# A spectral mixer and a gated feed-forward on one core: two transform stages and the first batch in plain float32, the weights' conversion on VectorE, mixed rows moved from SBUF to SBUF

## The chip, the cores and the metric

One core of a Trainium2 chip runs the whole program. The core has five engines that the text speaks of by the profile's names: PE (TensorE, which multiplies matrices; PEld is its loading of the stationary operand), DVE (VectorE), ACT (ScalarE), POOL (GpSimd) and SP (SyncE, which here issues every DMA). The metric is device time in microseconds (us), the median of several executions.

## The reference

```python
X = np.fft.rfft(x, axis=1)                      # x: [8 batches, 3008, 256] float32
Yr = Xr @ w_r - Xi @ w_i + b_r
Yi = Xr @ w_i + Xi @ w_r + b_i
Y  = soft_threshold(Yr, 0.01) + 1j * soft_threshold(Yi, 0.01)
y  = np.fft.irfft(Y, n=3008, axis=1)            # [8, 3008, 256] = 24064 tokens of 256
h  = y @ w_in                                   # w_in: [256, 2048] float64
out = (h * sigmoid(1.702 * h)) @ w_out          # w_out: [2048, 256] float64, out float32
```

The two feed-forward weights come as float64 bits, and the kernel turns them into float32 on the chip.

## The kernel before

**Precision.** Almost every product is made of float32r operands, a float32 type of shorter mantissa that the PE multiplies in one pass. To keep float32's accuracy each operand is cut in two parts: `split(hi, lo, src)` (L124) lets ACT cast `src` into `hi` and lets DVE subtract, `lo = src - hi`. `mm3` (L128) then issues three matmuls into the same PSUM bank: hi x hi (L129), hi x lo (L130) and lo x hi (L131).

**The spectral part of one batch** (`spectral`) is a Fourier transform of 3008 = 64 x 47 points in steps:

- stage A (16 times a batch): `load_x`, `split_x`, then `stage_a`, the transform of length 47 as one `mm3` of 512 columns; the result goes through ACT to a DRAM buffer `s1`.
- stage B (12 times, each for a pair of k2): `load_b` reads a matrix `kr` and rows `br` of `s1`, `split_b` splits `br`, `stage_b` is the transform of length 64. The matrix `kbs` holds its high and its low part side by side, so that each of four products is one matmul of 256 columns (L272) and one of 128 (L273); the correction part of the bank is copied by ACT (L277) and added to the main part by DVE (L278).
- the mix (12 times): `stage_mix`, six `mm3` of 256 columns, then on DVE bias and threshold (L294 to L296), and on POOL the subtraction (L297). The rows `mv` are then written to a DRAM buffer `yd` (two DMAs) and read back as `yr` in another order of partitions (one DMA, `load_y`).
- the inverse of length 64 (12 times): `split_y`, then `stage_inv`, one `mm3` of 512 columns; ACT evicts it and it goes to the DRAM buffer `s2`.

**Tokens.** `load_u` reads 96 rows `ur` of `s2`, `split_u` splits them and `tokens(u)` (128 times in all) makes the last transform, of length 47, and 188 tokens at a time: four matmuls of 188 columns (L372) and four of 94 (L373) into two banks, ACT's copy (L375) and DVE's addition (L376) into `yf`, and a split of `yf` into the token tiles `th`, `tl`.

**Feed-forward.** For each of 47 tiles of 512 tokens and each of 8 quarters q of 256 hidden units, `Ffn.up` makes four `mm3` of 512 columns (`pa<-th,wi_h` and the like), the gate on ACT (L408), and splits `hb`/`lb` and `ht`/`lt`; `Ffn.down` makes seven `mm3` of 256 columns into the accumulator `po`. That is 12 matmuls of 512 columns and 21 of 256 for each of 376 pairs of tile and quarter.

**The weights' conversion** runs once at the start, for each q `up_weights` and `down_weights` (two halves). `from_float64` (L166) loads 512 KB of float64 and turns the bits: DVE L177, L178, L180 and L183, ACT L179 and L184, and on POOL two multiplications (L182, L185). `up_weights` adds a subtraction and an addition on POOL (L193, L194); `down_weights` six sums on POOL (L202 to L207) and a split.

**Order.** Each engine runs its own instructions strictly in the order in which the program's scheduler put them; a waiting instruction holds up what stands behind it on its engine. The program first runs all of batch 0's spectral part; the weights of q = 0 to 4 are converted meanwhile, and those of q = 5 to 7 are held back until the last mix of batch 0 (`tc.issue_after(mixed[0, 11])`, L461). Then follow four stage A of batch 1, the first three calls of `tokens`, and the feed-forward, in which the spectral parts of batches 1 to 7 fill in. PSUM has four banks that all but `po` share (`bank`, L115). In SBUF, seven tiles with the tag `w2` serve most of the spectral part.

Of the kernel before, what the change touches and what calls it, by code (L numbers as in the profile page):

```python
# [37 lines left out]
def halves(v):  # L38
    """v as the sum of two values of 12 significant bits."""
    def r12(u):  # L40
        m, e = np.frexp(u)
# [4 lines left out]


def constants():
# [7 lines left out]
    # DFT-47: rows (n2, p), columns (k2, re | im, p)  # L56
# [5 lines left out]
    # +1 where the bin of (k1, k2) is kept by rfft, -1 where its conjugate is  # L62
# [24 lines left out]
    # inverse DFT-47: rows (k2, re | im, p), columns (p, n2)  # L87
# [5 lines left out]

    pack = np.zeros((128, 928), np.float32)
    pack[:96, 0:192] = np.concatenate(halves(a), 1)
    pack[:, 192:704] = np.concatenate([h[i] for h in halves(np.stack([binv, binv0])) for i in range(2)], 1)
    pack[:96, 704:892] = np.concatenate(halves(ai), 1)
    pack[:, 892:916] = 1.0
    pack[N1:, 892:916] = sign
# [4 lines left out]
def fourier_mix_then_gated_ffn(ctx: ExitStack, tc: tile.TileContext, x, w_r, w_i, b_r, b_i, w_in, w_out, pack, kbs, out):  # L104
# [37 lines left out]
    wf_h = cst.tile([128, 3, 2, D], F32R, name="wf_h")
    wf_l = cst.tile([128, 3, 2, D], F32R, name="wf_l")

    def later_constants():
# [8 lines left out]
        split(wf_h[:, 2], wf_l[:, 2], wr)
        for i, op in ((0, ALU.add), (1, ALU.subtract)):
            t = buf2("wd")
            nc.vector.scalar_tensor_tensor(t, wr, -1.0, wi, ALU.mult, op)
# [8 lines left out]
    def from_float64(src):  # L166
        """(a, e): a + e is the float64 value; below float32's normal range -> 0."""
# [8 lines left out]
        v = nc.vector  # L176
        v.tensor_scalar(a, w1, 3, 0x3FFFFFF8, ALU.logical_shift_left, ALU.bitwise_and)  # L177
        v.scalar_tensor_tensor(a, w1, -0x40000000, a, ALU.bitwise_and, ALU.bitwise_or)  # L178
        nc.scalar.activation(m, w1f, AF.Abs)  # L179
        v.tensor_scalar(m, m, TINY, None, ALU.is_ge)  # L180
        af, ef = a.bitcast(F32), e.bitcast(F32)
        nc.gpsimd.tensor_tensor(af, af, m, ALU.mult)  # L182
        v.tensor_scalar(e, a, -0x800000, None, ALU.bitwise_and)  # L183
        nc.scalar.activation(m, w0, AF.Copy, scale=2.0 ** -52)  # L184
        nc.gpsimd.tensor_tensor(ef, ef, m, ALU.mult)  # L185
        return af, ef

    def up_weights(q):
# [4 lines left out]
        nc.gpsimd.tensor_tensor(a, a, hi.bitcast(F32), ALU.subtract)  # L193
        nc.gpsimd.tensor_tensor(lo, e, a, ALU.add)  # L194
# [349 lines left out]
```

## Time and profile before

| | |
|---|---|
| median of 3 runs | 2728.8 us (2728.42 to 2730.14) |
| span of the profiled execution | 2728.8 us |
| mean granted PE clock of the profiled execution | 0.983 |
| PE busy | 2614.7 us (96%), 16624 matmuls |
| DVE busy | 2333.5 us (86%) |
| ACT busy | 1830.1 us (67%) |
| POOL busy | 314.0 us (12%) |

The profiled execution's time is its span, 2728.8 us, and there is nothing around it that the page shows. An engine's busy time is the union of its instructions. Matmuls overlap each other in the record, so what one matmul costs is read from the distance of two starts, not from its duration.

### The profile page before, as it was taken

The page shows a single profiled execution, that of the slowest core. Times are in us where ns is not written, and L with a number is a line of the kernel's source. Part 1 is how long each engine was busy: PE and PEld are TensorE (multiplying, and loading weights), DVE is VectorE, ACT ScalarE, POOL GpSimd, SP SyncE. Part 2 cuts the span into 40 slices and gives each one's busy share as a digit, 9 for nine tenths or more (in the row PEclk, how much of TensorE's full clock was granted, in tenths as well). Part 3 has the DMA queues.
Part 4 walks back from the last instruction along what each step waited for, and adds up shares of the span by engine and source line. Part 5 has one row for each costly group of instructions (what it writes and reads, how often), then busy time and mean ns, then how long its engine had stood idle before and what let it go on. Part 6 is the DMA issues. An engine that isn't in the chain of part 4 may idle for free.

```text
span 2728.8 us, 44465 instructions
## 1 busy us (share of the span) xinstructions
PE 2614.7 (96%) x16624; PEld 2351.6 (86%) x16624; DVE 2333.5 (86%) x3885; ACT 1830.1 (67%) x3190; POOL 314.0 (12%) x243
## 2 busy tenths in 40 slices
PE   4759999999999999999999999999999999999998
PEld 2639988899889998899988998889998898999997
DVE  7988998889888988789888999879898799877776
ACT  6557667767677666766668666766667666666564
POOL 6660110010000100001000100000010011000000
PEclk9769999999999999999999999999999999999999
DMA  6553334223242222422233222322224223200000
GB/s 212 165 158 101 92 89 117 89 83 86 67 126 81 83 82 78 123 77 75 75 108 110 68 75 80 118 86 79 76 79 130 72 68 91 82 30 31 17 22 16
DMA packets 181897, 238.53 MB, mean 87 GB/s; under 512 B 17200, under 2 KB 116272, under 8 KB 181680
## 3 DMA queue, kind: packets, MB, share of 16 engines
q1 hardware_dynamic: 181680, 235.69, 29.5%
q8 instruction: 130, 2.13, 0.3%
q14 instruction: 87, 0.71, 0.1%
HBM read 135.48 MB, written 100.14 MB: 86 GB/s over the span
## 4 chain that ended last, share of the span: by engine, by line
PE 62%; DVE 2%; ACT 1%; issue 1%; DMA 0%; DVEq 0%; SPq 0%; ACTq 0%
PE pa L129 11%; PE pa L130 11%; PE pa L131 11%; PE po L129 8%; PE po L130 8%; PE po L131 8%; PE pa L372 1%; PE pa L272 1%; PE pa L373 1%; ACT gb L408 0%; PE pa L273 0%; DVE gt L417 0%; DVE lt L126 0%; ACT hb L125 0%; DVE lb L126 0%
## 5 line engine op out<-in xcount | busy, mean ns | idle before, releaser
L408 ACT ACTIVATE gb<-pa 128x512 f32<-128x512 f32 x752 | 445.5, 597 | 417.7 <-PE pa L131 414.3
L129 PE MATMUL pa<-th,wi_h 128*128 128x512 f32 x1504 | 595.7, 396 | 9.8 <-ACT th L125 4.3
L126 DVE TENSOR_TENSOR lt<-gt,ht 128x1024 fp32r<-128x1024 f32 x376 | 465.8, 1239 | 161.3 <-ACT ht L125 160.5
L130 PE MATMUL pa<-tl,wi_h 128*128 128x512 f32 x1504 | 591.3, 393 | 0.0
L131 PE MATMUL pa<-th,wi_l 128*128 128x512 f32 x1504 | 588.1, 391 | 0.0
L125 ACT CAST ht<-gt 128x1024 fp32r<-128x1024 f32 x376 | 394.5, 1049 | 109.0 <-DVE gt L419 105.3
L130 PE MATMUL po<-lt,wo_h 128*128 128x256 f32 x1504 | 430.7, 286 | 1.2 <-DVE lt L126 1.2
L129 PE MATMUL po<-ht,wo_h 128*128 128x256 f32 x1504 | 428.7, 285 | 0.9 <-ACT ht L125 0.9
L131 PE MATMUL po<-ht,wo_l 128*128 128x256 f32 x1504 | 426.4, 283 | 0.0
L126 DVE TENSOR_TENSOR lb<-gb,hb 128x768 fp32r<-128x768 f32 x376 | 365.2, 971 | 68.9 <-ACT hb L125 66.0
L125 ACT CAST hb<-gb 128x768 fp32r<-128x768 f32 x376 | 314.6, 837 | 68.6 <-PE po L131 64.8
L129 PEld LDWEIGHTS pa<-th,wi_h 128*128 128x128 f32 x1504 | 284.0, 189 | 61.9 <-ACT gb L408 6.8
L129 PE MATMUL po<-hb,wo_h 128*128 128x256 f32 x1128 | 325.1, 288 | 11.0 <-DVE o L443 8.5
L131 PEld LDWEIGHTS pa<-th,wi_l 128*128 128x128 f32 x1504 | 283.2, 188 | 59.3
L130 PEld LDWEIGHTS pa<-tl,wi_h 128*128 128x128 f32 x1504 | 284.2, 189 | 43.4
L131 PE MATMUL po<-hb,wo_l 128*128 128x256 f32 x1128 | 320.5, 284 | 0.0
L130 PE MATMUL po<-lb,wo_h 128*128 128x256 f32 x1128 | 320.4, 284 | 0.0
L297 POOL TENSOR_TENSOR mv<-mv,mt 128x512 f32<-128x512 f32 x96 | 154.7, 1611 | 1322.2 <-DVE mt L296 1094.8
L417 DVE TENSOR_TENSOR gt<-gb 128x512 f32<-128x512 f32 x376 | 270.7, 720 | 33.7 <-ACT gb L408 28.8
L130 PEld LDWEIGHTS po<-lt,wo_h 128*128 128x128 f32 x1504 | 288.3, 192 | 9.3 <-DVE lt L126 1.6
L131 PEld LDWEIGHTS po<-ht,wo_l 128*128 128x128 f32 x1504 | 288.4, 192 | 7.1
L129 PEld LDWEIGHTS po<-ht,wo_h 128*128 128x128 f32 x1504 | 287.7, 191 | 7.7 <-ACT ht L125 1.1
(95 smaller groups left out, 5155.6 us busy)
## 6 DMA issues: line engine op xcount, KB each, us to landing
xr<-in_x SPq DMA_DIRECT2D x128, 192.0 KB, 3.1
kr<-in_kbs SPq DMA_DIRECT2D x96, 256.0 KB, 2.9
s<-aev SPq DMA_DIRECT2D x128, 192.0 KB, 2.3
br<-s SPq DMA_DIRECT2D x96, 256.0 KB, 3.0
yd<-mv SPq DMA_DIRECT2D x192, 128.0 KB, 2.4
yr<-yd SPq DMA_DIRECT2D x96, 256.0 KB, 2.9
s<-iev SPq DMA_DIRECT2D x96, 256.0 KB, 2.2
ur<-s SPq DMA_DIRECT2D x128, 192.0 KB, 2.8
```

What stands on the lines that cost most here:

```text
L125: nc.scalar.copy(hi, src)
L126: return nc.vector.tensor_tensor(lo, src, hi.bitcast(F32), ALU.subtract)
L129: nc.tensor.matmul(ps, lhsT=wh, rhs=xh, start=start, stop=False)
L130: nc.tensor.matmul(ps, lhsT=wh, rhs=xl, start=False, stop=False)
L131: nc.tensor.matmul(ps, lhsT=wl, rhs=xh, start=False, stop=stop)
L272: nc.tensor.matmul(pv[:, c, :], lhsT=bh[:, i, cs], rhs=kb[:, i], start=True, stop=False)
L297: nc.gpsimd.tensor_tensor(v, v, t, ALU.subtract)
L372: nc.tensor.matmul(pv[:, j, :], lhsT=uh[:, j, cs], rhs=kz, start=True, stop=False)
L373: nc.tensor.matmul(pv[:, j, :94], lhsT=ul[:, j, cs], rhs=kz[:, :94], start=False, stop=True)
L408: nc.scalar.activation(o, ps.rearrange("p (h n) -> p h n", h=2), AF.Gelu_apprx_sigmoid)
L417: nc.vector.tensor_tensor(gt[:, 0:2], b12, gb[:, 0:3:2], ALU.subtract)
```

## The change

Four things change.

1. **Batch 0's spectral part is made of plain float32 matmuls**: stage A, stage B, the mix and the inverse take the float32 tiles as they are, without `split` and with one matmul for each `mm3`. In `split_y` only ACT's scaling by the sign is left. The float32r parts of the constants are made for the later batches in `split_constants`.
2. **Stage B and `tokens` are plain float32 in every batch**: stage B is four matmuls of 128 columns into one bank, `tokens` four matmuls of 94 columns into one bank; the correction parts, their copies and additions, and the splits of `br` and `ur` are gone. `tokens` splits its PSUM bank straight into `th`, `tl`. The matrix `kr` is half as large.
3. **The weights' conversion** keeps on POOL only the six sums of `down_weights`. The comparison and multiplication that were L180 (DVE) and L182 (POOL) become one fused DVE instruction (new L186); L185, L193 and L194 become DVE instructions (new L190, L198, L199).
4. **Mixed rows** go from `mv` to `yr` by four DMAs from SBUF to SBUF; `yd` and `load_y` are gone.

```diff
 def later_constants():
...
+        for tag, op in (("ht", ALU.add), ("th", ALU.subtract)):
+            t = buf([128, 2, D], F32, "wd", tag=tag)
             nc.vector.scalar_tensor_tensor(t, wr, -1.0, wi, ALU.mult, op)
+            wf32.append(t)
+        wf32.append(wr)
+
+    def split_constants():
+        split(ka[:, 0], ka[:, 1], ka32)
+        split(ki[:, 0], ki[:, 1], ki32)
+        for v in range(3):
+            split(wf_h[:, v], wf_l[:, v], wf32[v])
...
 def from_float64(src):
...
+        nc.scalar.activation(m, w1f, AF.Abs)
         v.tensor_scalar(a, w1, 3, 0x3FFFFFF8, ALU.logical_shift_left, ALU.bitwise_and)
         v.scalar_tensor_tensor(a, w1, -0x40000000, a, ALU.bitwise_and, ALU.bitwise_or)
-        nc.scalar.activation(m, w1f, AF.Abs)
-        v.tensor_scalar(m, m, TINY, None, ALU.is_ge)
         af, ef = a.bitcast(F32), e.bitcast(F32)
-        nc.gpsimd.tensor_tensor(af, af, m, ALU.mult)
+        v.scalar_tensor_tensor(af, m, TINY, af, ALU.is_ge, ALU.mult)
         v.tensor_scalar(e, a, -0x800000, None, ALU.bitwise_and)
+        m = buf([128, 2, 256], F32, "wm", tag="lt")
         nc.scalar.activation(m, w0, AF.Copy, scale=2.0 ** -52)
-        nc.gpsimd.tensor_tensor(ef, ef, m, ALU.mult)
+        v.tensor_tensor(ef, ef, m, ALU.mult)
...
 def up_weights(q):
...
-        nc.gpsimd.tensor_tensor(a, a, hi.bitcast(F32), ALU.subtract)
-        nc.gpsimd.tensor_tensor(lo, e, a, ALU.add)
+        nc.vector.tensor_tensor(a, a, hi.bitcast(F32), ALU.subtract)
+        nc.vector.tensor_tensor(lo, e, a, ALU.add)
...
 def stage_a(q):
...
-            mm3(ps[:96], ka[:, 0], ka[:, 1], *xs.pop(q))
+            if b == 0:
+                nc.tensor.matmul(ps[:96], lhsT=ka32, rhs=xs.pop(q), start=True, stop=True)
+            else:
+                mm3(ps[:96], ka[:, 0], ka[:, 1], *xs.pop(q))
...
 def stage_b(sp):
...
+            pv = bank().rearrange("p (c v i n) -> p c v i n", c=2, v=2, i=2)
             for i in range(2):
-                pv = bank().rearrange("p (c n) -> p c n", c=2)
                 for c in range(2):
                     cs = slice(128 * c, 128 * c + 128)
-                    nc.tensor.matmul(pv[:, c, :], lhsT=bh[:, i, cs], rhs=kb[:, i], start=True, stop=False)
-                    nc.tensor.matmul(pv[:, c, :128], lhsT=bl[:, i, cs], rhs=kb[:, i, :128], start=False, stop=True)
...
+                    nc.tensor.matmul(pv[:, c, :, i], lhsT=t[:, i, cs], rhs=k[:, i], start=True, stop=True)
+            nc.scalar.copy(co[:, :, 0:2], pv.rearrange("p c v i n -> p c v (i n)"))
             nc.vector.tensor_tensor(co[:, :, 2], co[:, :, 0], co[:, :, 1], ALU.add)
+            z = co.rearrange("p c v n -> p (c v) n")
+            if b == 0:
+                zs[sp] = z
+                return
...
 def stage_mix(sp):
...
+                    if b == 0:
+                        nc.tensor.matmul(ps, lhsT=z[:, 3 * c + v], rhs=wf32[v][:, c], start=c == 0, stop=c == 1)
+                    else:
...
             nc.gpsimd.tensor_tensor(v, v, t, ALU.subtract)
+            y = ys[sp] = buf2("yr")
             for i in range(2):
-                nc.sync.dma_start(yd[2 * sp + i].rearrange("r k e -> k r e"), v[64 * i:64 * i + 64])
-
-        def load_y(sp):
-            ys[sp] = buf2("yr")
-            nc.sync.dma_start(ys[sp], yd[2 * sp:2 * sp + 2].rearrange("s r k e -> (r k) s e"))
+                for r in range(2):
+                    nc.sync.dma_start(y[64 * r:64 * r + 64, i], v[64 * i:64 * i + 64, r])
...
 def stage_inv(sp):
...
+            if b == 0:
                 for i in range(2):
-                    mm3(pv[:, i], ki[:, 0, 1 - i], ki[:, 1, 1 - i], yh[:, i], yl[:, i])
+                    nc.tensor.matmul(pv[:, i], lhsT=ki32[:, sp == 0 and i == 0], rhs=y[:, i], start=True, stop=True)
...
 def tokens(u):
-        uh, ul = us.pop(u)
...
+        t = us.pop(u)
+        pv = bank()[:, :2 * JP].rearrange("p (c n) -> p c n", c=2)
         for c in range(2):
...
             for j in range(2):
...
+                nc.tensor.matmul(pv[:, c, 94 * j:94 * j + 94], lhsT=t[:, j, 128 * c:128 * c + 128], rhs=kz, start=True, stop=True)
...
-            split(th[:, :, at:at + n], tl[:, :, at:at + n], yf[:, :, o:o + n])
+            split(th[:, :, at:at + n], tl[:, :, at:at + n], pv[:, :, o:o + n])
```

On PE, one call of `tokens` in the feed-forward, before (uh and ul are the parts of the loaded rows, kz the transform's matrix):

```order
L372 MATMUL pa<-kz,uh 128x188
L373 MATMUL pa<-kz,ul 128x94
L372 MATMUL pa<-kz,uh 128x188
L373 MATMUL pa<-kz,ul 128x94
L372 MATMUL pa<-kz,uh 128x188
L373 MATMUL pa<-kz,ul 128x94
L372 MATMUL pa<-kz,uh 128x188
L373 MATMUL pa<-kz,ul 128x94
L129 MATMUL pa<-th,wi_h 128x512
```

and in the changed kernel, between a mix and the feed-forward (kc is the tile of constants, ur the loaded rows):

```order
L131 MATMUL pa<-wf_l,zh 128x256
L132 MATMUL pa<-wf_h,zl 128x256
L370 MATMUL pa<-kc,ur 128x94 x4
L131 MATMUL po<-lb,wo_h 128x256
L132 MATMUL po<-hb,wo_l 128x256
```

Eight float32r matmuls of 188 and 94 columns became four float32 matmuls of 94; stage B's eight (256 and 128 columns) became four of 128 in the same way.

On POOL, the weights of q = 5 behind the last mix of batch 0, before (wa, we and wm are `from_float64`'s a, e and m; w is `down_weights`' tile):

```order
L297 TENSOR_TENSOR mv<-mv,mt 128x512 x8
L182 TENSOR_TENSOR wa<-wa,wm 128x512 x2
L185 TENSOR_TENSOR we<-we,wm 128x512
L193 TENSOR_TENSOR wa<-wa,wi_h 128x512
L185 TENSOR_TENSOR we<-we,wm 128x512
L194 TENSOR_TENSOR wi_l<-we,wa 128x2x256
L202 TENSOR_TENSOR w_1414<-we,wa 128x2x128
L202 TENSOR_TENSOR w_1414<-we,wa 128x256
```

and on DVE at that place in the changed kernel:

```order
L298 TENSOR_TENSOR mv<-pa,mv 128x512
L183 TENSOR_SCALAR wa<-wraw 128x512 x2
L299 TENSOR_SCALAR mt<-mv 128x512
L184 SCALAR_TENSOR_TENSOR wa<-wraw,wa 128x512 x2
L186 SCALAR_TENSOR_TENSOR wa<-wm,wa 128x512
L187 TENSOR_SCALAR we<-wa 128x512
L190 TENSOR_TENSOR we<-we,wm 128x512
L198 TENSOR_TENSOR wa<-wa,wi_h 128x512
L186 SCALAR_TENSOR_TENSOR wa<-wm,wa 128x512
L199 TENSOR_TENSOR wi_l<-we,wa 128x2x256
L187 TENSOR_SCALAR we<-wa 128x512
```

The six multiplications, subtractions and additions of a q that POOL made now stand in DVE's queue: six instructions more there, and two (L180) fewer. In the changed order the weights of q = 0 to 2 and most of q = 3 also stand ahead of the first addition of stage B (new L275) on DVE.

More of the change, by code (lines that the diff above doesn't have):

```diff
@@ L71, in constants @@
     b = np.stack([np.block([[c, -s * sign[:, k]], [s, c * sign[:, k]]]) for k in range(NS)])
-    b = np.stack(halves(b), 2).reshape(NS // 2, 2, 2 * N1, 4 * N1).transpose(0, 2, 1, 3)
+    b = b.reshape(NS // 2, 2, 2 * N1, 2 * N1).transpose(0, 2, 1, 3)
     w0r, w0i = np.zeros(N1), np.zeros(N1)
@@ L92, in constants @@
     ai = ai.reshape(96, 94)
[L94 to L99, printed above, removed]
+    pack = np.zeros((128, 470), np.float32)
+    pack[:96, 0:96] = a
+    pack[:, 96:224] = binv
+    pack[:, 224:352] = binv0
+    pack[:96, 352:446] = ai
+    pack[:, 446:470] = 1.0
+    pack[N1:, 446:470] = sign
     return pack, b.astype(np.float32)
@@ L249, in load_b, with stage_b @@
             raw[sp] = t, k
[L251 removed]
+        def stage_b(sp):
             if sp == 0:
@@ L315, in stage_inv @@
         def stage_inv(sp):
-            yh, yl = ys.pop(sp)
+            y = ys.pop(sp)
             pv = bank().rearrange("p (s d) -> p s d", s=2)
-            if sp == 0:
+            if b == 0:
                 for i in range(2):
-                    mm3(pv[:, i], ki[:, 0, 1 - i], ki[:, 1, 1 - i], yh[:, i], yl[:, i])
+                    nc.tensor.matmul(pv[:, i], lhsT=ki32[:, sp == 0 and i == 0], rhs=y[:, i], start=True, stop=True)
+            elif sp == 0:
+                for i in range(2):
+                    mm3(pv[:, i], ki[:, 0, 1 - i], ki[:, 1, 1 - i], y[0][:, i], y[1][:, i])
             else:
-                mm3(pv, ki[:, 0, 0], ki[:, 1, 0], yh, yl)
+                mm3(pv, ki[:, 0, 0], ki[:, 1, 0], *y)
             ev = buf2("iev")
@@ L336, in spectral @@
         steps.append((4000, lambda: None))
-        for n in range(12 + 5):
-            add(0, split_b, n, 12)
+        for n in range(12 + 4):
             add(900, stage_b, n, 12)
             add(2000, stage_mix, n - 1, 12)
-            add(0, load_y, n - 3, 12)
-            add(0, split_y, n - 5, 12)
-            add(650, stage_inv, n - 5, 12)
+            add(0, split_y, n - 4, 12)
+            add(650, stage_inv, n - 4, 12)
         return steps
@@ L468, in fourier_mix_then_gated_ffn @@
             spec.pop(0)[1]()
-    done, ready = 0, 0
+    done = 0
     def tokens_to(n):
-        nonlocal done, ready
+        nonlocal done
         while done < NB * NU and JP * done < n:
-            while ready < min(done + 2, NB * NU) and JP * ready < n:
-                load_u(ready + 1)
-                split_u(ready)
-                ready += 1
+            load_u(done)
+            load_u(done + 1)
             tokens(done)
```

79 lines of the change are left out of this document (25 added, 54 removed).

## The prediction

> **What bounds the kernel now.** I read the 40 slices of the page first, then the chain that ended last, then the stretches of the start, then who makes PE wait.
>
> ```profile
> PE   4759999999999999999999999999999999999998
> POOL 6660110010000100001000100000010011000000
> PE 62%; DVE 2%; ACT 1%; issue 1%; DMA 0%; DVEq 0%; SPq 0%; ACTq 0%
> ```
>
> From the fourth slice on PE is full and the last chain is PE alone; in the first three PE is half idle and POOL is busy. The stretches (each row: length, then busy time of PE, PEld, DVE, ACT, POOL, granted clock):
>
> ```profile
> 0.00:55.60 55.60, 25.59 (x48) 11.36 (x48) 41.91 (x47) 32.85 (x59) 38.09 (x32) 1.00 0.74 229
> 55.60:143.00 87.40, 63.57 (x339) 56.26 (x339) 85.45 (x129) 49.93 (x97) 53.15 (x44) 0.84 0.57 164
> 143.00:191.00 48.00, 20.60 (x49) 11.26 (x50) 44.37 (x53) 26.36 (x52) 40.27 (x33) 0.53 0.55 164
> ...
> 250.00:2728.80 2478.80, 2445.94 (x15851) 2221.39 (x15849) 2116.16 (x3583) 1674.27 (x2903) 179.11 (x131) 1.00 0.27 80
> ```
>
> Two regimes, then. From 250 us PE is idle for 2478.8 - 2445.9 = 33 us in all. Before 191 us DVE is the fullest engine (85.45 of 87.4 in batch 0's stages B to inverse), and in the third stretch POOL with DVE. The rows that mark the stretches: on PE the first stage B, the last inverse and the first feed-forward matmul; on DVE the first weight instruction and the last mix; on POOL the first weight work after that mix, and the end of it.
>
> ```profile
> 55.64 0.79 PE L272 MATMUL pa<-kb,bh 128*128 128x256 f32 x2 [7.87 <-ACT bh L125]
> 157.19 0.79 PE L129 MATMUL pa<-yh,ki 128*128 128x512 f32 x1 [3.71 <-ACT yh L311]
> 190.77 1.22 PE L129 MATMUL pa<-th,wi_h 128*128 128x512 f32 x2 [4.26 <-ACT th L125]
> ```
>
> ```profile
> 13.02 0.42 DVE L177 TENSOR_SCALAR wa<-wraw 128x512 int32<-128x512 int32 x1
> ...
> 143.61 0.68 DVE L295 TENSOR_TENSOR mv<-pa,mv 128x512 f32<-128x512 f32 x1
> ```
>
> ```profile
> 148.66 2.86 POOL L182 TENSOR_TENSOR wa<-wa,wm 128x512 f32<-128x512 f32 x2
> 194.13 0.46 POOL L207 TENSOR_TENSOR w<-w 128x128 f32<-128x128 f32 x1
> ```
>
> The last three q take POOL from 148.7 to 194.6, 15.3 us each, and the feed-forward begins under their end. So the change has two terms: how much earlier than 190.8 the feed-forward can begin, and what PE's work costs after it, where nearly every microsecond counts.
>
> **Term 1, the start.** POOL's rows for the weights:
>
> ```profile
> L185 POOL TENSOR_TENSOR we<-we,wm 128x512 f32<-128x512 f32 x16 | 25.9, 1619 | 4.2 <-DVE we L183 2.5 <-ACT co L277 1.3 <-ACT wm L179 0.4
> L182 POOL TENSOR_TENSOR wa<-wa,wm 128x512 f32<-128x512 f32 x16 | 24.5, 1535 | 22.7 <-DVE wm L180 15.6 <-DVE wa L178 5.6 <-DMA kr<-in_kbs 1.4
> L194 POOL TENSOR_TENSOR wi_l<-we,wa 128x512 fp32r<-128x512 f32 x8 | 13.8, 1719 | 0.1
> L193 POOL TENSOR_TENSOR wa<-wa,wi_h 128x512 f32<-128x512 f32 x8 | 12.2, 1530 | 0.0
> ```
>
> These 76.4 us of 131.5 (the three stretches) leave POOL; 55 us stay. What they cost on DVE I bound by DVE's means in the start, while POOL is busy, and by single instructions and steady means without it:
>
> ```profile
> L178 DVE SCALAR_TENSOR_TENSOR wa<-wraw,wa 128x512 int32<-128x512 int32 x16 | 14.5, 910 | 0.2
> L183 DVE TENSOR_SCALAR we<-wa 128x512 int32<-128x512 int32 x16 | 14.8, 929 | 1.2 <-POOL wa L182 1.2
> L177 DVE TENSOR_SCALAR wa<-wraw 128x512 int32<-128x512 int32 x16 | 11.2, 697 | 0.6 <-POOL w L202 0.6
> L126 DVE TENSOR_TENSOR wo_l<-w,wo_h 128x896 fp32r<-128x896 f32 x8 | 11.3, 1418 | 0.9 <-ACT wo_h L125 0.9
> L126 DVE TENSOR_TENSOR xl<-xr,xh 96x512 fp32r<-96x512 f32 x30 | 28.5, 963 | 11.0 <-ACT xh L125 11.0
> ...
> 37.73 0.41 DVE L183 TENSOR_SCALAR we<-wa 128x512 int32<-128x512 int32 x1
> ...
> L126 DVE TENSOR_TENSOR bl<-br,bh 128x512 fp32r<-128x512 f32 x81 | 55.4, 684 | 11.8 <-ACT bh L125 11.5
> ...
> L296 DVE TENSOR_SCALAR mt<-mv 128x512 f32<-128x512 f32 x14 | 5.8, 417 | 0.0
> ```
>
> A q is now two of each of L177, L178, the fused one (not in the trace; priced as L178, also a fused instruction on the same shape), L183 and L190, and one each of L198, L199 and the split. With POOL busy: 2 x (0.70 + 0.91 + 0.91 + 0.93 + 0.96) + 2 x 0.96 + 1.42 = 12.2 us. Without: 2 x (0.41 + 0.68 + 0.68 + 0.41 + 0.68) + 2 x 0.68 + 1.0 = 8.1 us (1.0: the split's 1.42 scaled as 0.963 goes to 0.684). POOL's share of the start falls from 131.5/191 = 69% to about 55/146 = 38%, so I take 9.5, somewhat nearer the lower bound. The Trainium skill (SBUF — State Buffer, SBUF: two separate sides) has VectorE and GpSimd taking turns at a shared port, the loser blocked for the whole instruction. The 0.41 beside a mean of 0.93 agrees; by that rule POOL's remaining 55 us are the most that DVE can lose.
>
> Now in DVE's order:
>
> 1. *To stage B.* The first weight instruction ran at 13.0 us, after the first load; the constants' three subtractions and two fused sums cost 3 x 0.96 + 2 x 0.91 = 5 us; ahead of the first new L275 stand 7.6 halves of 4.75 us = 36. Sum 54 us (bounds 49 to 64). Stage A is covered: it loses `split`, PE needs 16 x 0.92 = 15 us, and only its evictions and loads remain, interleaved with the weights on ACT. Without that cover its way through `s1` would show, which is the 7.87 us that PE waits ahead of 55.64.
> 2. *Twelve pairs.* DVE per pair: an addition of at most 0.68 and the mix, 2 x 0.68 + 0.42, 2.5 us, times 12 plus 2.4 halves of weights = 41. PE per pair, by the prices of term 2: 4 x 0.23 + 6 x 0.46 + 2 x 0.46 = 4.6, times 12 = 55, plus 2 to fill: last mix at 111 us against 143.6 now. PE takes over as the bound here. (At a clock of 0.84 it would be 9 us more; with PE full I expect 1.00, as after 200 us.)
> 3. *To the feed-forward.* Three q of 9.5 us plus six `xl` of 0.68 = 33: 144, and some 2 us of `tl` and the first matmul: 146. Under this cover lies the last pair's way to `s2` and back: now the last inverse begins 157.2 - 143.6 = 13.6 us after the last mix, with the two DMA steps below in it; one fewer (2.9), the inverse (0.9) and two more such steps (5.3) make 17 us, which would show only if the weights took less than that.
>
> The SBUF to SBUF exchange drops one of two DMA steps:
>
> ```profile
> yd<-mv SPq DMA_DIRECT2D x192, 128.0 KB, 2.4
> yr<-yd SPq DMA_DIRECT2D x96, 256.0 KB, 2.9
> ```
>
> SP issues four DMAs for three; the first waits for POOL as `yd`'s did, with the next `kr`, `br` and `s2` behind it. Later batches read `yr` long after; I price it at 0 beyond the 17 us above.
>
> Term 1: 146 - 191 = **-45 us**. With lower bounds everywhere (49 + 2, the pairs at DVE's 39, then 24 + 4 + 2): 120, -71; with upper bounds (64 + 57 + 5 for the clock, then 37 + 4 + 2): 169, -22.
>
> **Term 2, PE after the start.** Starts of float32r matmuls in the steady part, two neighbours of 512 and of 256 columns, and the ends of a `tokens` half and of a stage B:
>
> ```profile
> 1012.74 0.40 PE L129 MATMUL pa<-th,wi_h 128*128 128x512 f32 x1
> 1012.97 0.39 PE L130 MATMUL pa<-tl,wi_h 128*128 128x512 f32 x1
> ...
> 1015.04 0.28 PE L131 MATMUL po<-ht,wo_l 128*128 128x256 f32 x1
> 1015.16 0.28 PE L129 MATMUL po<-ht,wo_h 128*128 128x256 f32 x1
> ...
> 1010.07 0.25 PE L372 MATMUL pa<-kz,uh 96*128 96x188 f32 x1
> 1010.63 0.28 PE L130 MATMUL po<-lb,wo_h 128*128 128x256 f32 x1
> ...
> 1017.17 0.28 PE L272 MATMUL pa<-kb,bh 128*128 128x256 f32 x1
> 1018.21 0.28 PE L129 MATMUL po<-hb,wo_h 128*128 128x256 f32 x1
> ```
>
> 512 columns cost 0.23, 256 cost 0.12. Between 1010.07 and 1010.63 lie four `tokens` matmuls and one of 256: 0.56 - 0.12 = 0.44, 0.11 each though they have 188 or 94 columns. Stage B's eight: 1.04 - 0.12 = 0.92, 0.115 each. So below 256 columns the price is that of a stationary load, about 0.115, whatever the columns. What a plain float32 matmul costs no row shows. From below: one load and pass, 0.115. From above: four products of halves, each with its own load, 0.46. Between: two loads (high and low stationary half), 2 x 0.115 = 0.23; and four products by columns at 128 are 512 columns, also 0.23. I take 0.23 for 128 and 94 columns, and by columns 0.46 for 256 and 0.92 for 512.
>
> Stage B: 4 x 0.23 = 0.92 against 0.92: 0 for 84 pairs. `tokens`: 0.92 against 0.88, 125 times: +5 us. Bounds: one load, -(0.46 x 84 + 0.42 x 125) = -91; four, +(0.92 x 84 + 0.96 x 125) = +197.
>
> The Trainium skill (FP8 and Floating Point Precision, TensorE Precision Notes) counts four passes of the array for true FP32; read as columns that is the sum taken, read as four whole matmuls it is the first rival.
>
> **Term 3, waits of PE.** DVE loses, after 250 us,
>
> ```profile
> L126 DVE TENSOR_TENSOR ul<-ur,uh 96x512 fp32r<-96x512 f32 x121 | 82.7, 684 | 0.7 <-ACT uh L125 0.3
> L376 DVE TENSOR_TENSOR yf<-pa,yf 128x188 f32<-128x188 f32 x244 | 78.6, 343 | 4.0 <-ACT yf L375 3.8
> L278 DVE TENSOR_TENSOR co<-pa,co 128x256 f32<-128x256 f32 x166 | 66.9, 417 | 13.5 <-ACT co L277 13.0
> ```
>
> and `bl`'s 55.4: 284 of 2116 us. That is off PE's path; it can shorten only the 33 us in which PE waits. I take a quarter, -8 (bounds 0 and -33).
>
> Sum against the profiled 2728.8, which is also the median: 2728.8 - 45 + 5 - 8 = **2681 us**.
>
> **Rivals.**
>
> *Float32 costs PE more than 0.23 below 256 columns.* The place is stage B and `tokens` in the full part, 836 matmuls; the gain of 48 is gone when each costs 48/836 = 0.06 more, at 0.29. For it: a stationary load's own record is 0.19 (192 ns) against a step of 0.115,
>
> ```profile
> L130 PEld LDWEIGHTS po<-lt,wo_h 128*128 128x128 f32 x1504 | 288.3, 192 | 9.3 <-DVE lt L126 1.6
> ```
>
> and two halves could fail to hide behind each other: 0.38 each gives (1.52 - 0.92) x 84 + (1.52 - 0.88) x 125 = +130 in place of +5: 2806. Four loads give 2873. Against it: loads of float32r overlap well. Chance 0.17.
>
> *VectorE's conversion stays at its slow means.* For it: POOL's sums and subtractions still run beside it. Term 1 -22: 2704. Chance 0.18.
>
> *The start shrinks further and the waits go:* weights at 8.1 us a q, but the pairs still at PE's 55 (49 + 2 + 55 + 30 = 136, -55), and term 3 at -28: 2651. For it: DVE's single instructions of 0.41. Against it: DVE would then be next to full for 130 us, with ACT's casts between its steps. Chance 0.12.
>
> *One load suffices for float32:* 2728.8 - 45 - 91 - 8 = 2585. Against it: then splitting would gain nothing, and the halves' products must come from somewhere. Chance 0.03.
>
> **How the numbers follow.** The forecast has 0.48, and 0.02 stay for a float32 price close to 0.29, no change. Faster by over 0.2% (5.5 us, about what a measurement tells from no change): 0.48 + 0.18 + 0.12 + 0.03 = 0.81; the same 0.02; slower 0.17. The range reaches from 2640, midway between the third rival and all lower bounds together (2728.8 - 71 + 5 - 33 = 2630), to 2735, into the first rival; below it lies some 0.06, above it 0.14.
>
> **What would show it.** First feed-forward matmul near 146 us; last mix near 111; DVE full from 111 to 144. Four L370 or L273 followed by the next matmul within 0.92 + 0.12 us. PE idle after the start about 25 us, DVE near 1850. Wrong if the groups of four float32 matmuls take over 1.2 us, or if the feed-forward begins after 170 us.

## The result and the profile after

The changed kernel takes **2644.6 us** (median of 4 runs, 2643.55 to 2644.80) against 2729.5 for the kernel before, run beside it (4 runs, 2728.42 to 2730.44): ratio **0.9689**, 95% interval 0.9675 to 0.9703, or 85 us less. The forecast was 48 us less. The profiled execution has a span of 2642.9 us and a mean granted clock of 0.986; below, spans are compared with spans.

The slices and the chain of the changed kernel's page:

```profile
PE   6799999999999999999999999999999999999998
POOL 3401110001000100000100100000100010000000
PE 94%; DVE 2%; DMA 1%; ACT 1%; issue 1%; SPq 0%; POOL 0%; DVEq 0%; ACTq 0%; POOLq 0%
```

PE is now full from the third slice on, and POOL does little even at the start. I cut both traces at the first feed-forward matmul. The kernel before, the two stretches (length, then busy time of PE, PEld, DVE, ACT, POOL with their instructions, granted clock, DMA share, GB/s):

```profile
0.00:190.77 190.77, 109.53 (x436) 78.65 (x436) 171.49 (x229) 109.02 (x207) 131.27 (x107) 0.81 0.61 183
190.77:2728.80 2538.03, 2505.17 (x16189) 2272.99 (x16189) 2162.04 (x3657) 1721.10 (x2984) 182.77 (x137) 1.00 0.28 80
```

The changed kernel, the start in its three steps (to the first stage B, to the last mix, to the feed-forward), then the rest:

```profile
0.00:45.00 45.00, 23.94 (x33) 7.00 (x33) 31.62 (x51) 25.30 (x43) 12.97 (x20) 0.72 0.90 283
45.00:105.50 60.50, 54.99 (x274) 47.29 (x275) 40.68 (x69) 27.81 (x51) 24.66 (x26) 0.93 0.60 171
105.50:138.60 33.10, 17.88 (x52) 10.50 (x50) 31.07 (x48) 20.62 (x37) 13.57 (x17) 0.60 0.71 215
138.60:2642.90 2504.30, 2487.87 (x16189) 2264.40 (x16189) 1904.69 (x3030) 1530.00 (x2357) 170.32 (x134) 1.00 0.23 68
```

So the 86 us between the spans are two amounts: the feed-forward begins **52 us** earlier (138.6 against 190.8), and the part after it is **34 us** shorter (2504.3 against 2538.0) with the same number of matmul records, 16189. Half of these 34 is PE's idle time (32.9 to 16.4), half is PE's busy time (2505.2 to 2487.9). In both kernels 6.2 us of the idle time come after the last matmul, so the gaps between matmuls fell from 26.7 to 10.2 us.

The marks of the start in the changed kernel's timeline, on PE the first stage B, the last inverses, the first `tokens` and the first feed-forward matmul:

```profile
44.93 3.76 PE L273 MATMUL pa<-kr,br 128*128 128x128 f32 x16 [9.87 <-DMA br<-s]
...
113.35 2.17 PE L327 MATMUL pa<-yf,kc 128*128 128x256 f32 x4 [2.79 <-ACT yf L312]
...
132.05 5.44 PE L370 MATMUL pa<-kc,ur 96*128 96x94 f32 x24
138.62 1.22 PE L130 MATMUL pa<-th,wi_h 128*128 128x512 f32 x2 [1.14 <-ACT th L126]
```

then ACT's first copy of stage B, and on DVE the first addition of stage B and the last mix:

```profile
47.69 0.58 ACT L274 COPY co<-pa 128x512 f32<-128x512 f32 x1
...
49.49 0.41 DVE L275 TENSOR_TENSOR co<-co 128x256 f32<-128x256 f32 x1
...
105.43 0.69 DVE L298 TENSOR_TENSOR mv<-pa,mv 128x512 f32<-128x512 f32 x1 [0.34 <-PE pa L292]
```

In the full part, a group of four plain float32 matmuls and what follows it, first a stage B, then `tokens` (each of the four stands as two records):

```profile
188.74 1.06 PE L273 MATMUL pa<-kr,br 128*128 128x128 f32 x8
189.56 0.36 PE L130 MATMUL po<-hb,wo_h 128*128 128x256 f32 x1
189.76 0.28 PE L131 MATMUL po<-lb,wo_h 128*128 128x256 f32 x1
...
1008.26 1.03 PE L370 MATMUL pa<-kc,ur 96*128 96x94 f32 x8
1009.07 0.36 PE L131 MATMUL po<-lb,wo_h 128*128 128x256 f32 x1
1009.27 0.28 PE L132 MATMUL po<-hb,wo_l 128*128 128x256 f32 x1
1009.39 0.28 PE L130 MATMUL po<-hb,wo_h 128*128 128x256 f32 x1
```

The stage B here holds PE from 188.74 to 189.56, 0.82 us, and `tokens` from 1008.26 to 1009.07, 0.81 us: 0.20 a matmul. The first float32r matmul after a group then takes 0.20 instead of 0.12.

Where did the 34 us lie? The table adds, for each kind of work, the time from each PE record's start to the next one's start, after the first feed-forward matmul (us; in brackets the gaps in which PE was idle, each put down to the record ahead of it; e2, e6 and e12 are experiments below):

```
                records   before        changed       e2            e6            e12
feed-forward up    4512  1053.6 (8.3)  1052.8 (7.7)  1060.1 (11.5) 1049.7 (6.1)  1052.3 (8.3)
feed-forward down  7896   977.5 (7.3)   965.7 (2.3)   967.8 (2.1)   968.4 (2.1)   977.2 (7.3)
stage A             324    78.5 (1.1)    77.2 (0.1)    77.3 (0.1)    76.9 (0.0)    77.1 (0.0)
stage B             672    77.6 (3.7)    68.3 (0.0)    67.5 (0.0)    68.4 (0.0)    77.6 (3.7)
mix                1512   183.7 (0.8)   181.5 (0.0)   182.7 (0.9)   182.5 (0.0)   183.8 (0.8)
inverse             273    60.0 (0.2)    57.9 (0.0)    58.7 (0.0)    58.4 (0.0)    59.5 (0.4)
tokens             1000   107.1 (5.2)   100.8 (0.0)   101.3 (0.4)   100.2 (0.0)   106.6 (5.0)
sum                      2538.0        2504.2        2515.5        2504.5        2534.1
```

Stage B and `tokens` together are 15.6 us shorter, but 8.9 of these were gaps; the feed-forward's second product, whose matmuls nobody touched, is 11.8 us shorter. Of these 11.8, 5.0 were gaps, and most of the rest was the granted clock (the share of its full clock that PE was given). In the kernel before, behind one of PE's waits:

```profile
1094.11 0.36 PE L129 MATMUL po<-hb,wo_h 128*128 128x256 f32 x1 [2.12 <-ACT xh L125]
...
1094.54 0.29 PE L129 MATMUL po<-hb,wo_h 128*128 128x256 f32 x1
1094.66 0.39 PE L130 MATMUL po<-lb,wo_h 128*128 128x256 f32 x1
1094.85 0.42 PE L131 MATMUL po<-hb,wo_l 128*128 128x256 f32 x1
1095.06 0.41 PE L129 MATMUL po<-hb,wo_h 128*128 128x256 f32 x1
```

and the stretch that begins there, granted clock 0.50:

```profile
1094.66:1098.07 3.41, 3.41 (x19) 3.41 (x18) 2.90 (x7) 1.44 (x2) 0.00 (x0) 0.50 0.65 206
```

The starts go from 0.12 to 0.21 us apart, with no gap, and this reads as busy time. The kernel before has three such stretches in the full part, at 1094.7, 1814.9 and 2142.6 us, 13.7 us in all, each right behind or within one of its three longest pauses there (2.1, 2.5 and 5.2 us); the changed kernel has one, 3.4 us, behind one of its two longest (2.1 us). The clock of the start also reaches past the first feed-forward matmul, by 6.2 us before and by 4.0 in the changed kernel.

Start by start, against the usual distance of the same kind of matmul in the same trace, the 33.8 us are: 16.5 of gaps; 4.0 because a record ahead of a gap runs its whole length where the next start would else come sooner (40 gaps before, 15 after); 5.0 of half clock; 2.6 of starts that come late without a gap; and 5.6 of the pace of undisturbed matmuls, of which stage B has 4.2.

What PE waited for, after 200 us, in two rows of the kernel before and the same two of the changed kernel (total, times, longest):

```profile
PE po L129 <- DVE o L443: 8.5, 3, 5.2
PE pa L129 <- ACT gb L408: 4.4, 7, 0.7
...
PE pa L130 <- ACT gb L402: 2.8, 4, 0.7
PE po L130 <- DVE o L437: 2.1, 1, 2.1
```

The largest part of the gaps, 8.5 us, was a wait for DVE to finish combining the feed-forward's accumulators (`o`, L443), which fell to 2.1.

### The profile page after: what moved, and what is told of

It reads as the page before. It is cut to its first block, busy times and chain, and to the rows that moved or that the text cites. A ratio compares the mean times of both kernels' runs of the same rounds, so it can differ in the third digit from the quotient of the medians.

```text
span 2642.9 us, 43152 instructions
## 1 busy us (share of the span) xinstructions
PE 2584.7 (98%) x16545; PEld 2329.2 (88%) x16545; DVE 2008.1 (76%) x3195; ACT 1603.7 (61%) x2488; POOL 221.5 (8%) x195
## 4 chain that ended last, share of the span: by engine, by line
PE 94%; DVE 2%; DMA 1%; ACT 1%; issue 1%; SPq 0%; POOL 0%; DVEq 0%; ACTq 0%; POOLq 0%
PE pa L130 17%; PE pa L131 17%; PE pa L132 17%; PE po L130 12%; PE po L131 12%; PE po L132 12%; PE pa L370 4%; PE pa L273 3%; PE pa L292 1%; DMA xr<-in_x 1%; DMA yr<-mv 0%; DVE wa L186 0%; ACT gb L402 0%; DVE wa L184 0%; DMA wraw<-in_w_in 0%
## 5 line engine op out<-in xcount | busy, mean ns | idle before, releaser
L127 DVE TENSOR_TENSOR lt<-gt,ht 128x1024 fp32r<-128x1024 f32 x376 | 484.6, 1289 | 260.0 <-ACT ht L126 259.0
L300 POOL TENSOR_TENSOR mv<-mv,mt 128x512 f32<-128x512 f32 x96 | 146.1, 1522 | 1340.2 <-DVE mt L299 1071.7
```

The lines of the kernel that those rows point to most:

```text
L127: return nc.vector.tensor_tensor(lo, src, hi.bitcast(F32), ALU.subtract)
L300: nc.gpsimd.tensor_tensor(v, v, t, ALU.subtract)
```

## The experiments

My theory after the result: the start's 52 us come from the conversion on VectorE and from batch 0's float32 together, and the 34 us after it from float32 in stage B and `tokens`, mostly by less waiting. The rivals: one of the two alone sets the start; float32's price on PE makes the 34 us; or the exchange does.

**e6, the steady part alone.** On the kernel before, only this, and for batch 0's tile `kb` two buffers instead of one:

```diff
-    bh/bl split, 4 x (256 + 128 columns) float32r, copy, two additions   # stage B, batches 1 to 7
+    4 matmuls of 128 columns, float32, one copy
-    uh/ul split, 4 x (188 + 94 columns) float32r, copy, addition         # tokens
+    4 matmuls of 94 columns, float32
```

> The kernel before with plain float32 stage B in batches 1 to 7 and plain float32 `tokens`, and nothing else: batch 0, the weights' conversion and the exchange through DRAM stay as before, three low buffers stay. Theory (float32 gives the 34 us after the start, as PE's work and as idle time): PE's part after the start 2504 us, the start within 3 us of 191: 2729.5 - 34 = 2695 us. The prediction's prices (+5, -8): 2726 us. If the gain after the start needs the exchange: 2729 us.

Measured 2689.6 us, ratio 0.9856 (0.9842 to 0.9871). The feed-forward begins at 183.8, and the part after it, in e6:

```profile
183.77:2688.20 2504.43, 2490.00 (x16189) 2267.19 (x16189) 1906.03 (x3031) 1523.80 (x2357) 177.49 (x140) 1.00 0.26 77
```

2504.4 us, as in the changed kernel. So float32 in these two stages makes the whole 34 us by itself, without the exchange, and without the other edits of the change. It began the feed-forward 7 us earlier, where 3 were allowed for; in the start `tokens` and the buffers of `kb` differ from the kernel before, and which of them it is was not tried.

**e1, e5, e9, e12, the start alone.** The changed kernel with float32r stage B (batches 1 to 7) and `tokens`. e1 has the change's two buffers of low parts; e5 has three, as before; e5 makes room by putting the constants' tile elsewhere; e9 also sends the mixed rows through DRAM again; e12 also puts the inverse back from four to five steps behind its stage B.

```diff
e1  -4 float32 matmuls  +split, 8 float32r matmuls, copy, addition   # stage B (batches 1 to 7), tokens
e5  -buf([...], F32R, "xl", tag="sl")   +buf([...], F32R, "xl", tag="sl", bufs=3)   # and yl, bl, ul
e9  -dma_start(y[64*r:..., i], v[64*i:..., r])   +dma_start(yd[2*sp+i], v[...]); load_y at n - 2
e12 -add(0, split_y, n - 4, 12); add(650, stage_inv, n - 4, 12)
    +add(0, split_y, n - 5, 12); add(650, stage_inv, n - 5, 12)      # load_y at n - 3
```

> Stage B of batches 1 to 7 and `tokens` in all batches go back to float32r splits, as in the kernel before; the start keeps its change. Theory after the result (a start shorter by 52 us, and 34 us after it, of which half is PE's work and half its idle time): the feed-forward still begins near 139 to 141 us, the rest of PE is 34 us longer, 2678 us. The prediction's prices (float32 costs PE 5 us more after the start, waits give 8): 2644.6 + 3 = 2648 us. If everything came from the start: 2645 us.

> Like e1_start_only (stage B of batches 1 to 7 and `tokens` in float32r, the start with its change), but with three buffers for the low parts as in the kernel before instead of two; the constants' tile moves into the ring of the high parts to make room. In e1 PE's part after the start took 2601 us, 63 more than in the kernel before, though its matmuls are the same there. Theory A (the third low buffer was missing): that part falls to 2538 us as before, in all near 2688 us. Theory B (the exchange from SBUF to SBUF holds a tile of the ring w2 from the mix on, and in float32r `kr` and `yf` stand in that ring too, so the rings run short): it stays near 2600, in all near 2748 us.

> Like e5_start_only_3lo (float32r stage B in batches 1 to 7 and `tokens`, three low buffers, the start with its change), but the mixed rows go through DRAM again. In e5 PE's part after the start took 2574 us against 2538 in the kernel before, for the same matmuls. If the exchange from SBUF to SBUF is what costs them (a tile of w2 held from the mix on, one DMA more a pair): the part falls to 2538 us; with the 10 us that e7 lost at the start, 2722 - 36 + 10 = 2697 us. If something else of the change does: it stays near 2574, in all 2724 to 2734 us.

> Like e9_start_dram, and the inverse of a pair comes five steps behind its stage B again, its loaded rows two steps ahead of their use, as in the kernel before (the change has four). With this, all of batches 1 to 7 and of the feed-forward is as in the kernel before, in float32r; only the start has the change. In e9 PE's part after the start took 2560 us against 2538 before. If the shorter distance costs these 22 us: 2538 us, in all 2696 us. If not (the order that the scheduler gives the instructions, or another tile): near 2560, 2718 us.

Measured: e1 2749.7 (ratio 1.0070, 1.0053 to 1.0086), e5 2724.5 (0.9984, 0.9975 to 0.9993), e9 2718.0 (0.9956, 0.9940 to 0.9973), e12 2687.3 (0.9842, 0.9826 to 0.9858). Their parts after the first feed-forward matmul, e1:

```profile
148.09:2749.60 2601.51, 2530.22 (x16189) 2284.12 (x16189) 2152.86 (x3656) 1720.04 (x2983) 174.05 (x131) 0.99 0.24 70
```

e5:

```profile
148.74:2722.70 2573.96, 2517.09 (x16189) 2279.34 (x16189) 2147.15 (x3656) 1717.74 (x2983) 178.27 (x131) 0.99 0.24 71
```

e9:

```profile
156.64:2716.90 2560.26, 2512.01 (x16189) 2283.88 (x16189) 2150.14 (x3655) 1722.02 (x2983) 180.61 (x131) 0.99 0.27 80
```

e12:

```profile
151.48:2685.60 2534.12, 2502.18 (x16189) 2272.40 (x16189) 2159.44 (x3655) 1720.33 (x2983) 177.36 (x131) 1.00 0.28 80
```

I had taken e1 for a clean "start only", and it came out slower than the kernel before, far from all three times that I had named. The rest of the row explains it: 2601.5, 2574.0, 2560.3, 2534.1 us for the same matmuls. With float32r the change's other edits cost the steady part, undone in this order: the missing third low buffer 28 us, the exchange 14, the shorter distance of four steps 26. Theory A and B of e5 were each a part, and e9 fell between its two values. Only with all three undone does it stand near where it stood before (2538.0), and the table shows e12 within 1.5 us of the kernel before in each kind. With float32 none of these is felt: 2504.3 in the changed kernel, 2503.5 in e7 (exchange through DRAM) and 2504.4 in e6 (three low buffers, five steps, DRAM). So the start without its exchange is worth 42 us (e12) and float32 alone 40 (e6, the 7 at the start among them). The start's edits as they stand, with two low buffers, the exchange and four steps, paid only together with float32: with float32r they made the kernel 19 us slower than before (e1).

**e2, the load of the removed splits.**

```diff
+    bh, bl = buf(...), buf(...); split(bh, bl, t)   # stage B, b >= 1: results unread
+    uh, ul = buf(...), buf(...); split(uh, ul, t)   # tokens: results unread
```

> The changed kernel with the removed splits of `br` (batches 1 to 7) and `ur` put back on ACT and DVE, their results read by nobody; the float32 matmuls stay, so ACT and DVE have 138 us more each and PE's work is the same. If PE's waits after the start fell because these engines are less full: PE's idle time there goes from 16 back to about 33 us, 2661 us. If it fell because the chain from the load through a split to the matmul is shorter: 2645 us.

Measured 2659.4 us (0.9741, 0.9727 to 0.9756), 14.8 more than the changed kernel. The part after the start, in e2:

```profile
142.64:2658.10 2515.46, 2494.23 (x16189) 2267.59 (x16189) 2025.37 (x3238) 1616.46 (x2565) 175.08 (x131) 1.00 0.23 68
```

It is 11.2 us longer, of which PE's idle time is 4.8 (16.4 to 21.2) and its busy time 6.4; the other 4 us are at the start. The total hit the first theory's 2661 but not by its way: idle time did not go back to 33. Nor do the 11 us lie where the 34 lay. By the table 7.3 of them lie in the first product, which the change had shortened by 0.8; the second product, stage B and `tokens`, where 27 of the 34 lay, have 1.8. The two longest waits of e2 after 150 us:

```profile
PE pa L130 <- ACT gb L409: 8.1, 8, 1.8
PE po L130 <- DVE o L444: 2.4, 2, 2.1
```

It is the gate's result `gb` that comes late now, not `o`. And e2 puts back only part of what went: on DVE 121 of 257 us (2025.4 against 1904.7, and 2162.0 before), on ACT 86 of 191; the copies and additions behind the matmuls stay out. Its low parts also share the change's two buffers; with two instead of three e1 lost 28 us against e5. So e2 does not settle how much of the 34 us the load on ACT and DVE makes. What remains open is that load, the longer chain (split before the matmuls, copy and addition after them) and the buffers.

**e10, float32 where there are 256 columns.** The mix in float32 in all batches.

```diff
-    mm3(ps, z[0][:, 3*c+v], z[1][:, 3*c+v], wf_h[:, v, c], wf_l[:, v, c], ...)
+    nc.tensor.matmul(ps, lhsT=z[:, 3*c+v], rhs=wf32[:, v, c], ...)
```

> The changed kernel with the mix in plain float32 in all batches, not only in batch 0: six matmuls of 256 columns a pair in place of six groups of three float32r matmuls (0.36 us a group), and no split into `zh`, `zl`. If float32 costs by columns (0.43 us each, as the twelve records of 2.6 us in batch 0's pairs show): +0.07 x 6 x 84 = 35 us, less some 5 of waits, 2675 us. If it costs by loads (0.20 each whatever the columns): -0.16 x 504 = 81 less, 2564 us.

Measured 2678.1 us (0.9808, 0.9794 to 0.9823), 33 more than the changed kernel. A pair's mix in e10:

```profile
1014.68 2.75 PE L279 MATMUL pa<-wf,co 128*128 128x256 f32 x12
1017.08 0.47 PE L130 MATMUL po<-hb,wo_h 128*128 128x256 f32 x1
1017.38 0.28 PE L131 MATMUL po<-lb,wo_h 128*128 128x256 f32 x1
```

Six matmuls take 2.40 us, 0.40 each, and the next float32r matmul takes 0.30 instead of 0.12. That is 0.43 each against 0.36 for three float32r matmuls: 0.07 x 504 = 35, of which the part after the start shows 31 (2535.4 against 2504.3). So float32 costs by columns at 256. The price is 0.20 at 128 columns, half that of 256, and also 0.20 at 94 columns, where the columns no longer set it.

**e3, the conversion back on POOL.**

```diff
-    v.scalar_tensor_tensor(af, m, TINY, af, ALU.is_ge, ALU.mult)
+    v.tensor_scalar(m, m, TINY, None, ALU.is_ge); nc.gpsimd.tensor_tensor(af, af, m, ALU.mult)
-    v.tensor_tensor(ef, ...); nc.vector.tensor_tensor(a, ...); nc.vector.tensor_tensor(lo, ...)
+    nc.gpsimd.tensor_tensor(...)   # all three
```

> Only the weights' conversion goes back to the division of before (three multiplications and sums a half on POOL, the comparison apart from the multiplication). Theory (the weights' conversion carries over half of the start's gain): stage B begins near 55 us instead of 45, and the last three q take 15.3 us each instead of about 10, in all 10 + 17 = 27 us more, 2672 us. Rival (batch 0's float32 carries it, the conversion lies beside other work): under 2650 us.

**e4, batch 0 back to float32r** in stage A, mix and inverse.

```diff
-    if b == 0: nc.tensor.matmul(...)   # stage A, mix, inverse
+    mm3(...)                           # and split_x, zh/zl, yh/yl for batch 0; its br in two tiles, not four
```

> Stage A, the mix and the inverse of batch 0 go back to float32r splits; stage B and `tokens` stay float32, the conversion on VectorE and the exchange from SBUF to SBUF stay. Theory: DVE gets stage A's 16 splits at 0.7 to 0.96 us ahead of stage B (11 to 15 us) and per pair two more instructions of 1 and 1.4 us, and is again the bound of the twelve pairs: last mix near 130 us instead of 105, 2670 us. Rival (the weights alone set the start): under 2650 us.

Measured: e3 2657.5 us (0.9735, 0.9721 to 0.9750), 12.9 more than the changed kernel; e4 2662.2 us (0.9750, 0.9736 to 0.9765), 17.6 more. The last two steps of the start in e3 (its first stage B comes at 42.8, its last mix at 113.3):

```profile
42.78:113.30 70.52, 58.55 (x277) 50.12 (x278) 59.51 (x73) 32.23 (x59) 56.45 (x51) 0.89 0.60 171
113.30:151.35 38.05, 17.00 (x50) 9.88 (x48) 27.84 (x36) 20.44 (x37) 34.05 (x29) 0.59 0.63 185
```

and in e4:

```profile
48.14:122.94 74.80, 58.84 (x345) 49.73 (x345) 70.57 (x107) 38.41 (x66) 31.35 (x29) 0.88 0.56 153
122.94:155.61 32.67, 16.15 (x43) 9.49 (x43) 31.27 (x52) 20.57 (x37) 11.58 (x14) 0.52 0.72 215
```

In e3 the last step is 38.0 us instead of 33.1 and POOL is its fullest engine (34.05); in e4 DVE fills the pairs (70.6 of 74.8 us) and the last mix comes at 122.9. Neither rival holds: both edits were needed. Both cost less than I expected (27 and 25). In e3 stage B is not later at all (42.8), 8 of the 13 us are lost by the last mix already (113.3 instead of 105.4, with POOL busy for 56.45 of 70.52 us in the pairs), and the last three q take POOL about 34 / 3 = 11 us each, not 15.3.

**e7, the exchange back through DRAM.**

```diff
-    nc.sync.dma_start(y[64*r:64*r+64, i], v[64*i:64*i+64, r])   # four, y taken at the mix
+    nc.sync.dma_start(yd[2*sp+i], v[64*i:64*i+64])             # two, and load_y(n - 2)
```

> The changed kernel with the mixed rows exchanged through DRAM again (two DMAs out, one back, a tile for the rows only when they are loaded). The prediction priced the SBUF to SBUF exchange at 0 beyond the last pair's way: 2645 us within 3. If the way of the last pair had set the start: 2648 to 2650 us. If the exchange costs time after the start (it holds a tile longer and issues one DMA more a pair): under 2640 us.

Measured 2654.1 us (0.9729, 0.9713 to 0.9746), 9.5 more than the changed kernel; the feed-forward begins at 148.4, the part after it is 2503.5. My price of 0 was wrong. What waits, in e7's timeline, ACT after the last mix:

```profile
110.63 0.91 ACT L315 ACTIVATE yf<-yr,kc 128x256 f32<-128x256 f32 x2 [3.87 <-DMA yr<-yd]
...
115.58 0.91 ACT L315 ACTIVATE yf<-yr,kc 128x256 f32<-128x256 f32 x2 [3.57 <-DMA yr<-yd]
116.39 0.60 ACT L197 CAST wi_h<-wa 128x512 fp32r<-128x512 f32 x1
```

and DVE there:

```profile
111.99 0.69 DVE L190 TENSOR_TENSOR we<-we,wm 128x512 f32<-128x512 f32 x1
117.02 0.69 DVE L198 TENSOR_TENSOR wa<-wa,wi_h 128x512 f32<-128x512 f32 x1 [4.33 <-ACT wi_h L197]
```

The last pairs' scaling `yf` waits on ACT for their rows, the weights' cast `wi_h` stands behind it on ACT, and DVE stands still for 4.3 us for that cast. The last pair's way was not covered by the weights: by ACT's order it held the weights up. This standstill is 4.3 of the 9.8 us by which the feed-forward begins later; the last mix comes 1.5 us later (106.9), and the remaining 4 us were not traced.

**e8 and e11, tries at a better version.**

```diff
e8  -if q >= 5: held_back   +if q >= 6: held_back       # until the last mix
    -stage A of batch 1 (four) ahead of tokens          +behind the first three tokens
e11 -weights q = 5, 6, 7 held back until the last mix   +q = 5, 6; q = 7 until the third split of th
    -stage A of batch 1 (four), float32r, ahead         +float32, behind the first three tokens
```

> A try at a better version: of the weights only q = 6 and 7 wait for the last mix (q = 5 is free to fill DVE's idle time beside batch 0's pairs, where PE is the bound), and the first three `tokens` come ahead of batch 1's first four stage A. Theory (between the last mix at 105 and the feed-forward at 139 DVE is full with three q of weights and the splits of stage A): 8 to 14 us earlier, 2631 to 2637 us. Rival (q = 5 on DVE delays the mix by as much, or the moved splits come back as waits in the first tiles): 2642 to 2648 us.

> A second try at a better version: the weights of q = 5 and 6 wait for the last mix as before, those of q = 7 for the third split into the first token tile; the first three `tokens` come ahead of batch 1's first four stage A, and these four are plain float32, so that DVE has no splits for them there. Theory (DVE's 31 of 33 us between the last mix and the feed-forward set its start): 9.5 us of weights and 2.7 us of splits less ahead of the first feed-forward matmul, which comes at 126 to 130 us instead of 139; some of that returns as waits in the first steps: 2634 to 2640 us. Rival (the last pair's way through DRAM to the first tokens sets it, or all of it returns as waits): 2643 to 2648 us.

Measured: e8 2651.9 us (0.9718, 0.9703 to 0.9732), 7 us worse than the changed kernel and worse than its rival; e11 **2640.0 us** (0.9669, 0.9655 to 0.9684), 4.6 us better than it in the medians, though the two ratios' intervals overlap. In e8 the q that was let go early delayed the pairs; the stretch of the pairs, and the last mix:

```profile
45.00:112.88 67.88, 58.39 (x267) 49.26 (x267) 49.91 (x80) 31.41 (x57) 29.03 (x31) 0.85 0.58 165
...
112.88 0.69 DVE L298 TENSOR_TENSOR mv<-pa,mv 128x512 f32<-128x512 f32 x1 [0.51 <-PE pa L292]
```

The last mix came 7.5 us later, the feed-forward at 138.1, and stage A's waits came after it (2510.3 us for the rest). DVE's idle time beside the pairs was not free to fill, though DVE was not full with it (49.9 of 67.9 us). Whether it was the order on DVE, ACT's casts between the pairs' copies or the lower clock (0.85 instead of 0.93) that held the pairs up is not shown. In e11, PE from the first `tokens` on:

```profile
123.11 5.41 PE L370 MATMUL pa<-kc,ur 96*128 96x94 f32 x24 [7.52 <-DMA ur<-s]
129.57 5.82 PE L246 MATMUL pa<-xr,kc 96*96 96x512 f32 x8 [1.06 <-DMA xr<-in_x]
134.83 0.80 PE L130 MATMUL pa<-th,wi_h 128*128 128x512 f32 x1
```

`tokens` come 9 us earlier, but the feed-forward only 4, since four stage A stand ahead of it on PE. The rest took 2502.3 us, so nothing came back. The total is at the edge of what I expected, but the first feed-forward matmul came at 134.8, not at 126 to 130.

## Why the prediction was right, and where its sizes were off

The sign, the two regimes and the order of the gains held. The time, 2644.6, is 36 us under the forecast, only 4.6 us inside the range's lower end, and nearest to the third rival (2651: the start shrinks further and the waits go), which had a chance of 0.12. All three terms missed to the same side, by 7, 8 and 23 us; that their sum still fell into the range owes something to luck.

*What bounds it.* Right. The start gave 52 us, PE the rest.

*Term 1, the start: -45 forecast, -52 measured.* By its steps: the first L275 came at 49.5 instead of 54 (the q's means in the changed trace sum to 9.5 us, as taken, but neighbours' records overlap, and the constants cost less). DVE bounded this step only by a hair: ACT's copy ahead of L275 ended 1.2 us before it, and PE had waited 9.87 us for the rows `br`, so stage A's way through `s1` was not covered as forecast. The pairs took 56 us against 57, with PE the bound (55.0 busy of 60.5); from the last mix to the feed-forward 33.2 against 35, with DVE full (31.07 of 33.10). Expected granted clock 1.00, measured 0.93 in that stretch, so the pairs' PE price was taken a little high. Against the 8.1 us a q that the prediction worked out without POOL, 9.5 is a loss of 11 us over eight q. By the rule cited there (the Trainium skill, SBUF — State Buffer, SBUF: two separate sides) POOL's busy time, 51.2 us in this start, bounds what DVE loses; 11 us lies within that bound and tests it little.

*The exchange at 0.* This step failed. "17 us, which would show only if the weights took less than that" treats the last pair's way and the weights as two chains side by side. e7 shows that they share ACT, in order, and that the shorter way is worth 9.5 us. It did not show in the sum because the step to the feed-forward was priced as if DVE were never held up, which the exchange made true.

*Term 2, PE's price: +5 forecast, about -3 measured.* The medians over the whole steady part: a float32 group 0.81 and its successor 0.08 longer, 0.89, in stage B and in `tokens`; before, stage B 0.87 and a successor 0.05 longer, 0.92, and `tokens` two halves of 0.38, each with a successor 0.065 longer, 0.89. That is -0.03 x 84 for stage B and nothing for `tokens`. The model of two loads of 0.115 was right in kind: the trace shows two records with two loads for each float32 matmul. It was high by 0.03 a matmul, 0.12 a group, of which the successor takes 0.08 back. The first rival (0.29 or more) is out. The Trainium skill (FP8 and Floating Point Precision, TensorE Precision Notes) counts four passes for true FP32; read as columns it comes near what e10 shows at 256 columns, 0.43 with the successor's delay against 0.12 for one float32r matmul, a factor of 3.6; read as four whole matmuls with their loads it does not hold, since there are two.

*Term 3, the waits: -8 forecast, about -31 measured* (34 less the 3 of term 2). This is the term that was mis-sized, near its bound of -33. Two things in its step were wrong. A quarter was taken of PE's idle time, and half of it went (32.9 to 16.4); since 6.2 us of the 33 come after the last matmul, that is 16.5 of 26.7. And "it can shorten only the 33 us in which PE waits" was wrong: PE's busy time fell by 17.3 us with as many records. Of this, about 3 is term 2's price. The rest is mostly what comes with a wait and reads as busy: matmul records overlap (0.28 us long, 0.12 apart), so a wait costs some 0.16 us more than its gap, 4.0 us in sum; and the stretches at half clock, most of them behind long waits, cost 5.0 us more before than after. Starts that come late without leaving a gap are 2.6 us. e6 shows that the whole 34 us go with float32 alone. Whether they go by the smaller load on DVE and ACT, the shorter chain or the freed buffers was not tried apart; e2 does not settle it. That e1, e5 and e9 moved the float32r part by 14 to 28 us for each buffer or step of distance shows how near to late that chain ran.

*What would show it.* First feed-forward matmul 138.6 (near 146 said), last mix 105.4 (near 111), DVE full to the feed-forward (yes), groups within 1.04 us (1.02 and 1.01 to the second following start), PE idle after the start 16 (about 25), DVE after the start 1905, after 250 us 1821 (near 1850).

## What to carry to other kernels

Where a product has 128 columns or fewer, price a float32r split not by its matmuls alone: its loads cost as much as plain float32's, and it brings the splits, their buffers and a longer chain; at 256 columns the split was the cheaper one on PE. A busy share of 96% on an engine with overlapping records hides the end of each wait and whatever ran at a lower granted clock: compare starts, look at the clock where they draw apart, and count what a wait costs behind it as part of the wait. And before calling a transfer covered by other work, look in whose queue its consumer waits, and what stands behind it there.

## What the runs showed of the hardware

A plain float32 matmul stands in the trace as two matmul records, each with its own weight load: 0.10 us a record with 94 and with 128 columns, 0.20 with 256. The first float32r matmul behind such a group starts its successor late, 0.20 us instead of 0.12 behind 94 or 128 columns and 0.30 behind 256; I had not expected this: it adds 0.08 us to each group of `tokens` or stage B. In the full part the granted clock, 1.00 in the rows' mean, fell to 0.50 for 3.4 or 6.8 us at a time, with the starts of 256 columns 0.21 us apart instead of 0.12. In the kernel before each of the three stretches followed a pause of PE of over 2 us, and pauses of up to 1.0 us had none behind them; in the changed kernel one of two pauses of 2.1 us had one. The 16189 records of the full part took from 2487 (the changed kernel) to 2530 us (e1) of busy time. Between e1 and e12 (2530 and 2502) the matmuls are the same; half clock cost 23 us in e1 and 8 in e12, worked out from the starts as above.
